# Attention in chunks and a gated feed-forward on one core: the values product on eighths of the array, a third slot of streamed output weights, later ring loads, and a longer turn in tile two

## The chip, the cores and the metric

The kernel runs on one core of a Trainium2 chip. The time is device time in microseconds (us) of one execution: the median of three runs before the change was 960.36 us, and the runs went from 959.24 to 962.48 us. Five engines with a queue each work in parallel: TensorE (PE in the profile, with its weight loads as PEld), VectorE (DVE), ScalarE (ACT), GpSimd (POOL) and SyncE (SP), which here issues nearly every DMA transfer, in the order of its own queue.

## The reference

```python
# q, k, v: (8, 8, 576, 64), batch, heads, tokens, head dim
q_c = q.reshape(B, H, nc, 64, D)                 # chunks of 64 tokens
scores = scale * (q_c @ k_c.T)                   # 64 x 64 in each chunk and head
attn = softmax(scores)                           # over the 64 keys of the chunk
x = (attn @ v_c) -> (4608 tokens, 512)           # heads side by side
xn = x / sqrt(mean(x * x) + 1e-06) * rms_g
out = (silu(xn @ w_gate) * (xn @ w_val)) @ w_out # 512 -> 1536 -> 512, fp32
```

## The kernel before

There are 4608 tokens, in nine tiles of 512. Attention works in units of 256 tokens, two to a tile. A unit has two halves of 128 tokens (two chunks of 64), called subs below.

The feed-forward is done in split fp32: each operand is a high and a low part, and a product is three matmuls. One matmul of 128 x 128 weights on 512 columns is the kernel's unit of work on TensorE. Tiles 0 to 2 go through `gated` and `down` for each of 12 blocks of the hidden width: 24 matmuls of the up products and 12 of the down product a block. The last six tiles go in three pairs (b = 0, 1, 2). A pair's up products are done in seven part products on weights streamed from DRAM in a ring of three slots (`wr` from `wsd`, `ring_load_ahead`); then its down products run over 12 steps n, each with one streamed megabyte of output weights (`wo` from `wod`, `out_load`), which feeds 24 matmuls. All these slots, the hidden values `g`, the operands `xp` and the ring, come from one pool of 18 buffers.

Attention for later tiles is spread between the feed-forward's matmuls. The order on TensorE is written out by hand from tile 1 on, as numbered steps; the order on the other engines is set by a scheduler from the order of the code and priorities. A unit's steps are: load, scores and softmax (`turned_softmax`), sums and the first half of a turn (`turned_sum`, `turn`), the second half (`turn_back`), values and norm (`turned_values`, `turned_norm`), and the turn of the result to the feed-forward's layout (`turn_x`, `turn_x_back`). `UNIT_STEPS` and `PAIR_STEPS` say how many steps each stands behind the unit's first. In tiles 1 and 2 there are two steps a block (one before the down product of the block before, one behind it).

A turn makes the softmax weights `e` (tokens on partitions) into `eT` (keys on partitions), which the values product needs as its weights: VectorE transposes blocks of 32 x 32 in place, one DMA writes `e` to DRAM (`away_e`), and four DMAs a sub read it back in another order (eight a unit).

`e` is stored as (partition, half of the keys, 32 keys, 8 heads), so that for one head neighbouring keys lie 8 elements apart, and `eT` as (partition, 64 queries, 8 heads). The values product takes one head, one chunk of 64 queries and one sub at a time: 64 keys by 64 queries as weights, 64 columns of values, on a quarter of the array (64 rows by 64 columns), 32 products a unit. An fp32 product shows in the profile as two records, so a unit shows 64.

Tile 1, the second one, is called tile two here. Beside its units 4 and 5 it computes the sums of up weights that the part products need: `load` (`w` from `wfd`), `sums` on GpSimd (line 541), `split` (casts on ScalarE, line 569, subtractions on VectorE, line 571), and stores (`wsd` from `side` and `w`). At its end `x_split` (lines 442 and 443) makes the operands `xh` and `xl` of the next tile out of `x`, which units 4 and 5 have written.

Of the kernel before, what the change touches and what calls it, by code (L numbers as in the profile page):

```python
# [8 lines left out]
F32 = mybir.dt.float32  # L9
# [5 lines left out]
ALU = mybir.AluOpType  # L15
AX = mybir.AxisListType

P = 128
CH = 64
D = 64  # L20
H = 8
# [12 lines left out]
AHEAD = 4  # L34
EARLY = 3
AHEAD_R = 3

URGENT = 300
UNIT_AT = 1, 5, 9, 13
UNIT_STEPS = -2, 0, 1, 3, 5, 6, 7  # L40
PAIR_STEPS = -4, 0, 3, 5, 8, 11, 13
CONVS = (2,), (0, 2)
Q = 32
# [4 lines left out]
NB = (NT - PLAIN) // 2  # L48
# [13 lines left out]
def tile_chunk_attn_swiglu(  # L62
# [10 lines left out]
    nc = tc.nc  # L73
# [6 lines left out]
    att = ctx.enter_context(tc.tile_pool(name="att", bufs=2))  # L80
# [118 lines left out]
    state = {}  # L199
# [95 lines left out]

    def turned_softmax(i):
        st = state[i]
        e = st["e"] = att.tile([P, 2, Q, H], F32, tag="e", name="e")
        ev = e.rearrange("p t k (a j) -> p j a t k", j=2)
        mx = small.tile([P, 2, NPAIR, 1], F32, name="mx")  # L300
        for j in range(2):
            nc.vector.tensor_reduce(mx[:, j], st["s"][j], axis=AX.X, op=ALU.max)
            nc.vector.tensor_tensor(
                ev[:, j],
                st["s"][j].rearrange("p a (t k) -> p a t k", t=2),
                mx[:, j].rearrange("p a (o i) -> p a o i", i=1).broadcast_to([P, NPAIR, 2, Q]),
                op=ALU.subtract,
            )
        nc.scalar.activation(e, e, AF.Exp, scale=SCALE)

    def turned_sum(i):
        st = state[i]
        rs = st["rs"] = small.tile([P, H, 1], F32, name="rs")
        nc.vector.tensor_reduce(rs, st["e"].rearrange("p t k h -> p h t k"), axis=AX.XY, op=ALU.add)
        nc.vector.tensor_scalar_add(rs, rs, 1e-9)
        nc.vector.reciprocal(rs, rs)

# [2 lines left out]
    def turn(i):  # L320
        st, s = state[i], i % 2
        if s == 0:
            state["eT", i // 2] = [att.tile([P, 2 * Q, H], F32, tag="eT", name="eT") for _ in range(2)]
        eT = state["eT", i // 2]
        e = st["e"].rearrange("p t k h -> p t h k")
        nc.vector.transpose(e, e)
        away = st["away"] = dram.tile([P, 2 * Q * H], F32, name=f"away_e{i}")
        nc.sync.dma_start(away, st["e"].rearrange("p t k h -> p (t k h)"))

    def turn_back(i):  # L330
        st, s = state[i], i % 2
        eT, away = state["eT", i // 2], st["away"]
        back = away.rearrange("(c t p) (k r) -> c k p t r", c=2, t=2, k=2)
        for c in range(2):
            for k in range(2):
                dst = slice((2 * s + k) * Q, (2 * s + k + 1) * Q)
                nc.sync.dma_start(eT[c][dst].rearrange("p (t q) h -> p t (q h)", t=2), back[c, k])

    def turned_values(u):
        subs = [state[2 * u + s] for s in range(2)]
        for st in subs:
            st["o"] = bank(ps_a, "ps_o")
        vt = subs[0]["v"].rearrange("p a n d -> p (a n d)").rearrange("p (c h d) -> p c h d", c=2, d=D)
        eT = state.pop(("eT", u))
        for s, st in enumerate(subs):
            st["eT"] = eT[s]
        for h in range(H):
            for c in range(2):  # L350
                for s, st in enumerate(subs):
                    rows = slice(s * CH, (s + 1) * CH)
                    nc.tensor.matmul(  # L353
                        st["o"][c * CH : (c + 1) * CH, h * D : (h + 1) * D],
                        eT[c][rows, :, h],
                        vt[rows, c, h],
                        start=True,
                        stop=True,
                    )

    def turned_norm(i):
        st = state.pop(i)
        if i % 2 == 0:

            state["xu", i // 2] = io.tile([P, 4, NDT, 2, Q], F32, tag="io", name="xu")
        xs = state["xu", i // 2].rearrange("p q a s d -> p s (q a) d")[:, i % 2]
        nc.vector.tensor_tensor(
            xs.rearrange("p (h b) d -> p h b d", b=2),
            st["o"].rearrange("p (h b d) -> p h b d", b=2, d=Q),
            st["rs"].rearrange("p h (o i) -> p h o i", i=1).broadcast_to([P, H, 2, Q]),  # L370
            op=ALU.mult,
        )

        spent = st["eT"].rearrange("p q h -> p (q h)").rearrange("p (n d) -> p n d", d=Q)
        nc.scalar.mul(xs, xs, inv_rms(xs, spent))


# [427 lines left out]
    o = two_banks(ps_h, "ps_o")  # L805
# [25 lines left out]
    for t in range(PLAIN):  # L831
        if t == 1:
            ordered = tc.manual_schedule(engines={mybir.EngineType.PE})
            ordered.__enter__()
            at = {}
            for n, u in enumerate((4, 5)):
                for k, f in enumerate(unit_steps(u, x)):
                    at.setdefault(2 + 9 * n + UNIT_STEPS[k], []).append(f)
            half = Steps(at)
            st = last.open("st", 1)  # L840
            made = [[] for _ in range(NF + 2)]
            for i in range(NPR):
                steps = sides(i, st)
                made[max(2 * i - 1, 0)].append(steps[0])
                made[2 * i].append(steps[1])
                made[2 * i + 1].append(steps[2])
        elif t == 2:
            st = last.open("st2", 1)
            x2 = st.tile([P, NSUB, DM], F32, tag="x2", bufs=1, name="x2")
            at = {}  # L850
            for n, u in enumerate(range(2 * PLAIN, 2 * PLAIN + 4)):
                for k, f in enumerate(unit_steps(u, (x, x2)[n // 2])):
                    at.setdefault(max(UNIT_AT[n] + UNIT_STEPS[k], 0), []).append(f)
            x_first, x_both = x_sides(x, x2, st)
            for n, f in enumerate(x_first):
                at.setdefault(15 + n, []).append(f)
            for n, f in enumerate(x_both):
                at.setdefault(22 + n // 6, []).append(f)
            at.setdefault(14, []).append(lambda: ring_load_ahead(0))
            half = Steps(at)  # L860
        acc = [ps_acc.tile([P, DM], F32, tag="acc", name=f"acc{s}") for s in range(NSUB)]
        prev = None
        for f in range(NF):
            g = gated(f, CONVS[f % 2], conv_step)
            if t == 0:
                if f in (0, 5):
                    u = 2 + (f == 5)
                    load_unit(u)
                    sc = two_banks(ps_a, "ps_s")
                    for i in (2 * u, 2 * u + 1):  # L870
                        scores(i, sc)
                    for i in (2 * u, 2 * u + 1):
                        softmax_rows(i)
                elif f in (2, 7):
                    for i in (2 * u, 2 * u + 1):
                        att_transpose(i)
                elif f in (3, 8):
                    o = two_banks(ps_a, "ps_o")
                    for i in (2 * u, 2 * u + 1):
                        att_values(i, o)  # L880
                    for i in (2 * u, 2 * u + 1):
                        norm(i)
                if f == NF - 1:
                    x_transpose((0, 1))
            elif t == 1 and f == NF - 1:
                for dt in range(NDT):
                    x_split(dt, blocks(x)[:, :, dt], slice(0, TT))
            if t == 1:
                if f % 2 == 0:
                    save_plain(f // 2)  # L890
                for todo in made.pop(0):
                    todo()
            if t:
                half()
            if prev is not None:
                down(acc, f - 1, *prev)
            if t:
                half()
            prev = g
        if t == 0:  # L900
            x_transpose((2, 3))
        down(acc, NF - 1, *prev)
        for s in range(NSUB):
            evacuate(acc, t, s)

    for b in range(NB):
# [25 lines left out]
        for n, (h, i) in enumerate(order):  # L932
            if i == 0:

                acc = [bank(ps_h if h and s < 2 else ps_acc, f"acc{s}") for s in range(NSUB)]
            for k in range(n, min(n + 2, len(order))):
                if k not in wos:
                    wos[k] = out_load(order[k][1])
            if n == 1 and b + 1 < NB:
                ring_load_ahead(0)  # L940
            for j in range(2):
                split_next(2 * n + j + 1)
# [60 lines left out]
```

## Time and profile before

| | |
|---|---|
| median of 3 runs | 960.36 us |
| the profiled execution | 961.05 us, of which the profile's span is 959.3 us |
| TensorE busy | 922.0 us (96%) |
| VectorE, ScalarE, GpSimd busy | 547.9, 432.4, 172.9 us |
| DMA | 231.72 MB, 242 GB/s over the span |
| matmuls with 512 columns | 3672 |

A group row of the profile gives line, engine, operation, what is written from what, shapes, the count, then busy time and mean time of one, then the engine's idle time just ahead of these instructions with what ended it. A row of the chain or the timeline begins with the start and the duration in us. SPq rows are the times that the DMA queue needed to issue, not the transfers. Starts of TensorE records that follow each other closely are closer than their durations, since they are pipelined; the time that a burst costs is read from its first start to the first start behind it.

### The profile page before, as it was taken

To read this page: it belongs to the slowest core of one execution; us is meant where nothing else is said; L and a number is where in the kernel's file an instruction comes from. 1 tells how busy PE (TensorE), PEld (TensorE's weight loads), DVE (VectorE), ACT (ScalarE), POOL (GpSimd) and SP (SyncE) were. 2 spreads that over 40 slices of the span, in tenths; PEclk is the share of its full clock that TensorE was granted. 3 is DMA by queue.
4 is the path that set the end of the run, shared out by engine and by line. 5 is a ranking of instruction groups with operands and counts; after the bars stand their busy time and mean duration, and the time that the engine had idled before them with its cause. 6 is when DMAs were issued, how large, how long until landed. Compare 5 with 4: busy or idle time off the path is not lost.

```text
span 959.3 us, 15557 instructions
## 1 busy us (share of the span) xinstructions
PE 922.0 (96%) x6040; PEld 754.7 (79%) x6040; DVE 547.9 (57%) x889; ACT 432.4 (45%) x697; POOL 172.9 (18%) x157
## 2 busy tenths in 40 slices
PE   5699999998999999999999999999999999999998
PEld 4478788886888888888887788888786888888886
DVE  5899965673557655765673735557647333233232
ACT  4998954452446643553453424445424322222222
POOL 0100012342200000233341002323330004223100
PEclk9999999998999999999999999999999999999999
DMA  8698998877775544668789756576887666436611
GB/s 335 236 349 300 338 349 319 258 239 241 220 254 182 166 148 165 250 212 286 237 289 354 252 217 263 201 255 217 299 309 301 220 259 231 168 132 266 259 45 45
DMA packets 78730, 231.72 MB, mean 242 GB/s; under 512 B 8384, under 2 KB 40128, under 8 KB 62912
## 3 DMA queue, kind: packets, MB, share of 16 engines
q1 hardware_dynamic: 78656, 230.72, 67.7%
q8 instruction: 48, 0.79, 0.3%
q14 instruction: 26, 0.21, 0.1%
HBM read 171.97 MB, written 58.72 MB: 240 GB/s over the span
## 4 chain that ended last, share of the span: by engine, by line
PE 80%; ACT 6%; DMA 6%; DVE 4%; issue 1%; SPq 1%; POOL 0%; ACTq 0%; DVEq 0%; POOLq 0%
PE acc L503 26%; PE ps_b L634 10%; PE ps_c L634 10%; PE ps_a L634 10%; PE ps_g L468 8%; PE ps_v L468 7%; PE ps_d L634 5%; PE ps_o L353 3%; DMA wo<-wod 2%; PE ps_s L237 2%; DMA wfd<-w 1%; ACT w L150 1%; DMA vt<-v_dram 1%; ACT e L273 1%; ACT raw L151 1%
## 5 line engine op out<-in xcount | busy, mean ns | idle before, releaser
L503 PE MATMUL acc<-wo,gh 128*128 128x512 f32 x576 | 179.2, 392 | 4.7 <-DMA wo<-wod 4.7
L503 PEld LDWEIGHTS acc<-wo,gh 128*128 128x128 f32 x576 | 108.5, 189 | 28.6 <-ACT xp L582 5.1
L503 PE MATMUL acc<-wo,gl 128*128 128x512 f32 x288 | 113.4, 394 | 0.3 <-DVE gl L737 0.3
L737 DVE TENSOR_TENSOR gl<-g,gh 128x512 fp32r<-128x512 f32 x72 | 49.7, 690 | 105.2 <-ACT gh L736 103.2
L634 PE MATMUL ps_c<-xp,wr 128*128 128x512 f32 x432 | 104.4, 391 | 1.1 <-DMA wr<-wsd 1.1
L634 PE MATMUL ps_b<-xp,wr 128*128 128x512 f32 x432 | 104.6, 391 | 0.0
L634 PE MATMUL ps_a<-xp,wr 128*128 128x512 f32 x432 | 103.5, 390 | 0.0
L468 PE MATMUL ps_g<-xh,parts 128*128 128x512 f32 x288 | 97.1, 396 | 1.8 <-ACT sg L486 1.4
L736 ACT CAST gh<-g 128x512 fp32r<-128x512 f32 x72 | 44.8, 622 | 118.7 <-PE acc L503 113.4
L468 PE MATMUL ps_v<-xh,parts 128*128 128x512 f32 x288 | 95.8, 392 | 0.0
L634 PEld LDWEIGHTS ps_c<-xp,wr 128*128 128x128 f32 x432 | 80.7, 188 | 18.4 <-issue 1.5
L634 PEld LDWEIGHTS ps_a<-xp,wr 128*128 128x128 f32 x432 | 80.9, 188 | 16.9
L634 PEld LDWEIGHTS ps_b<-xp,wr 128*128 128x128 f32 x432 | 80.6, 188 | 17.0
L503 PE MATMUL acc<-parts,gh 128*128 128x512 f32 x288 | 91.5, 399 | 0.0
L708 POOL TENSOR_TENSOR g<-u,u 128x512 f32<-128x512 f32 x18 | 23.2, 1288 | 349.6 <-DVE u L704 207.1
L420 POOL TENSOR_TENSOR ri<-ss,mhalf 128x1 f32<-128x1 f32 x36 | 23.6, 664 | 252.6 <-DVE ss L418 252.3
L468 PEld LDWEIGHTS ps_g<-xh,parts 128*128 128x128 f32 x288 | 54.3, 189 | 14.3 <-ACT sg L486 1.8
L503 PEld LDWEIGHTS acc<-wo,gl 128*128 128x128 f32 x288 | 54.4, 189 | 13.5 <-DVE gl L737 1.9
L468 PEld LDWEIGHTS ps_v<-xh,parts 128*128 128x128 f32 x288 | 54.5, 189 | 11.4
L503 PEld LDWEIGHTS acc<-parts,gh 128*128 128x128 f32 x288 | 54.2, 191 | 11.4
L503 PE MATMUL acc<-parts,gl 128*128 128x512 f32 x144 | 57.2, 397 | 0.0
L468 PE MATMUL ps_g<-xl,parts 128*128 128x512 f32 x144 | 56.4, 392 | 0.0
(105 smaller groups left out, 1454.1 us busy)
## 6 DMA issues: line engine op xcount, KB each, us to landing
wr<-wsd SPq DMA_DIRECT2D x63, 1024.0 KB, 7.2
wo<-wod SPq DMA_DIRECT2D x36, 1024.0 KB, 7.7
raw<-w_up_dram SPq DMA_DIRECT2D x12, 1024.0 KB, 9.5
vt<-v_dram SPq DMA_DIRECT2D x18, 512.0 KB, 6.5
wsd<-parts SPq DMA_DIRECT2D x18, 512.0 KB, 6.8
out_dram<-o SPq DMA_DIRECT2D x36, 256.0 KB, 2.7
qt<-qT_dram SPq DMA_DIRECT2D x17, 512.0 KB, 6.5
kt<-kT_dram SPq DMA_DIRECT2D x17, 512.0 KB, 6.6
```

The costliest lines, as they stand in the source:

```text
L150: nc.scalar.activation(w, high.bitcast(F32), AF.Abs, scale=2.0**16)
L151: nc.scalar.mul(low, low.bitcast(U32), 2.0**-29)
L237: nc.tensor.matmul(st["s"][j][c * CH : (c + 1) * CH, pr], st["q"][rows, pr, tok : tok + CH], st["k"][rows, pr, tok : tok + CH], start=True ...
L273: nc.scalar.activation(e[:, pr, j], st["s"][j][:, pr], AF.Exp, scale=SCALE, bias=mx[:, j, pr], accum_out=rs[:, pr, j],)
L353: nc.tensor.matmul(st["o"][c * CH : (c + 1) * CH, h * D : (h + 1) * D], eT[c][rows, :, h], vt[rows, c, h], start=True, stop=True,)
L420: nc.gpsimd.tensor_tensor(ri, ss, mhalf, op=ALU.pow)
L468: nc.tensor.matmul(ps, a[f][:, cols], b[dt], start=(dt == 0 and i == 0), stop=(dt == NDT - 1 and i == 2),)
L503: nc.tensor.matmul(acc[s], a[:, cols], b, start=(f == 0 and i == 0), stop=(f == NF - 1 and i == 2),)
L634: nc.tensor.matmul(ps, w[:, a, m, cols], xp[:, b, kt], start=start and kt == 0 and i == 0, stop=stop and kt == 1 and i == 2, skip_group_ch ...
L708: nc.gpsimd.tensor_tensor(g[:, 0, 1], kp["u2"], kept[0]["u2"], op=mult)
L736: nc.scalar.copy(gh, src)
L737: nc.vector.tensor_tensor(gl, src, gh.bitcast(F32), op=ALU.subtract)
```

## The change

Four edits:

- The layouts of `e` and `eT` become (partition, half, 8 heads, 32), so that the 32 elements of one head are neighbours for the subtraction, the sum, the transposition and the weight load. The values product takes 32 queries at a time instead of 64, on an eighth of the array (64 rows by 32 columns): 64 products a unit.
- `AHEAD_O`: at step n of the down products the loads of output weights up to step n + 2 are written, before n + 1.
- The first loads of the next pair's ring are written at step 9 of the down products, before at step 1.
- `FIRST_STEPS`: in tile two, values, turn of the result and its way back stand two steps later.

```diff
+AHEAD_O = 3
 UNIT_STEPS = -2, 0, 1, 3, 5, 6, 7
+FIRST_STEPS = -2, 0, 1, 3, 7, 8, 9
...
     def turned_softmax(i):
-        e = st["e"] = att.tile([P, 2, Q, H], F32, tag="e", name="e")
-        ev = e.rearrange("p t k (a j) -> p j a t k", j=2)
+        e = st["e"] = att.tile([P, 2, H, Q], F32, tag="e", name="e")
+        ev = e.rearrange("p t (a j) k -> p j a t k", j=2)
...
     def turned_sum(i):
-        nc.vector.tensor_reduce(rs, st["e"].rearrange("p t k h -> p h t k"), axis=AX.XY, op=ALU.add)
+        nc.vector.tensor_reduce(rs, st["e"].rearrange("p t h k -> p h t k"), axis=AX.XY, op=ALU.add)
...
     def turn(i):
-            state["eT", i // 2] = [att.tile([P, 2 * Q, H], F32, tag="eT", name="eT") for _ in range(2)]
+            state["eT", i // 2] = [att.tile([P, 2, H, Q], F32, tag="eT", name="eT") for _ in range(2)]
-        e = st["e"].rearrange("p t k h -> p t h k")
+        e = st["e"].rearrange("p t h k -> p (t h) k")
         nc.vector.transpose(e, e)
...
     def turned_values(u):
         for h in range(H):
-            for c in range(2):
-                for s, st in enumerate(subs):
-                    rows = slice(s * CH, (s + 1) * CH)
-                    nc.tensor.matmul(
-                        st["o"][c * CH : (c + 1) * CH, h * D : (h + 1) * D],
-                        eT[c][rows, :, h],
+            for t in range(2):
+                for c in range(2):
+                    for s, st in enumerate(subs):
+                        rows = slice(s * CH, (s + 1) * CH)
+                        nc.tensor.matmul(
+                            st["o"][(2 * c + t) * Q : (2 * c + t + 1) * Q, h * D : (h + 1) * D],
+                            eT[c][rows, t, h],
                             vt[rows, c, h],
...
-                    at.setdefault(2 + 9 * n + UNIT_STEPS[k], []).append(f)
+                    at.setdefault(2 + 9 * n + FIRST_STEPS[k], []).append(f)
...
-            for k in range(n, min(n + 2, len(order))):
+            for k in range(n, min(n + AHEAD_O, len(order))):
                 if k not in wos:
                     wos[k] = out_load(order[k][1])
-            if n == 1 and b + 1 < NB:
+            if n == len(order) - AHEAD_R and b + 1 < NB:
                 ring_load_ahead(0)
```

First place: SyncE's queue in tile two, around the turn of unit 5. `away_e` is its write to DRAM, `eT<-away_e` its way back, `wsd` the stores of one group of summed weights. Before:

```order
L328 DMA away_e_2148<-e 128x512
L546 DMA w<-wfd_136 128x1024
L337 DMA eT<-away_e_2148 32x2x256
L328 DMA away_e_2155<-e 128x512
L337 DMA eT<-away_e_2148 32x2x256 x3
L337 DMA eT<-away_e_2155 32x2x256
L570 DMA wsd_153<-side 128x512
```

Now:

```order
L575 DMA wsd_152<-w 128x2x256
L549 DMA w<-wfd_137 128x1024
L339 DMA eT<-away_e_2180 32x2x256 x4
L339 DMA eT<-away_e_2187 32x2x256 x4
L549 DMA w<-wfd_138 128x1024
```

Before, five of the eight loads of `eT` stood ahead of the stores `wsd_153` to `wsd_152` and three behind them; now all eight stand behind the last of these stores. The stores themselves are the same eight.

Second place: ScalarE's queue at the end of tile two. `L442` (now `L445`) is the high part of `x_split`, `side<-w` are the casts of the last group of summed weights. Before:

```order
L486 ACTIVATE sg<-ps_g 128x512
L569 CAST side<-w 128x512
L442 ACTIVATE xh_119<-x,g_col 128x512
L442 ACTIVATE xh_120<-x,g_col 128x512
L442 ACTIVATE xh_121<-x,g_col 128x512
L442 ACTIVATE xh_122<-x,g_col 128x512
L569 CAST side<-w 128x512
L491 CAST gh<-sg 128x512
L569 CAST side<-w 128x512 x2
```

Now:

```order
L489 ACTIVATE sg<-ps_g 128x512
L572 CAST side<-w 128x512 x3
L494 CAST gh<-sg 128x512
L572 CAST side<-w 128x512
L445 ACTIVATE xh_119<-x,g_col 128x512
L445 ACTIVATE xh_120<-x,g_col 128x512
L445 ACTIVATE xh_121<-x,g_col 128x512
L445 ACTIVATE xh_122<-x,g_col 128x512
```

One of the four casts stood ahead of `x_split`; now all four and the cast `gh` of the last block do.

Third place: SyncE's queue at the beginning of the first pair's down products. `wo` are the output weights by their number in DRAM (161 to 166, twice), `wr` the ring of the next pair. Before:

```order
L742 DMA wo<-wod_162 128x2048
L742 DMA wo<-wod_163 128x2048
L626 DMA wr<-wsd_140 128x2048
L626 DMA wr<-wsd_141 128x2048
L626 DMA wr<-wsd_142 128x2048
L384 DMA away_x_5094<-xu 128x1024
L742 DMA wo<-wod_164 128x2048
L391 DMA x_2578<-away_x_5094 32x4x256 x4
L742 DMA wo<-wod_165 128x2048
```

Now (from the second load on, and then the end of the same phase's loads):

```order
L745 DMA wo<-wod_162 128x2048
L745 DMA wo<-wod_163 128x2048
L745 DMA wo<-wod_164 128x2048
L745 DMA wo<-wod_165 128x2048
L387 DMA away_x_5410<-xu 128x1024
L745 DMA wo<-wod_166 128x2048
L394 DMA x_2642<-away_x_5410 32x4x256 x4
```

```order
L733 DMA out_dram<-o 128x512 x4
L745 DMA wo<-wod_165 128x2048
L745 DMA wo<-wod_166 128x2048
L629 DMA wr<-wsd_140 128x2048
L629 DMA wr<-wsd_141 128x2048
L629 DMA wr<-wsd_142 128x2048
```

Two loads of output weights stood ahead of `away_x` and three ring loads with them; now four loads of output weights do, and the ring loads stand behind all twelve of the phase.

More of the change, by code (lines that the diff above doesn't have):

```diff
@@ L322, in turn @@
         if s == 0:
-            state["eT", i // 2] = [att.tile([P, 2 * Q, H], F32, tag="eT", name="eT") for _ in range(2)]
+            state["eT", i // 2] = [att.tile([P, 2, H, Q], F32, tag="eT", name="eT") for _ in range(2)]
         eT = state["eT", i // 2]
-        e = st["e"].rearrange("p t k h -> p t h k")
+        e = st["e"].rearrange("p t h k -> p (t h) k")
         nc.vector.transpose(e, e)
         away = st["away"] = dram.tile([P, 2 * Q * H], F32, name=f"away_e{i}")
-        nc.sync.dma_start(away, st["e"].rearrange("p t k h -> p (t k h)"))
+        nc.sync.dma_start(away, st["e"].rearrange("p t h k -> p (t h k)"))
     def turn_back(i):
@@ L336, in turn_back @@
                 dst = slice((2 * s + k) * Q, (2 * s + k + 1) * Q)
-                nc.sync.dma_start(eT[c][dst].rearrange("p (t q) h -> p t (q h)", t=2), back[c, k])
+                nc.sync.dma_start(eT[c][dst].rearrange("p t h q -> p t (h q)"), back[c, k])
     def turned_values(u):
@@ L349, in turned_values @@
         for h in range(H):
-            for c in range(2):
-                for s, st in enumerate(subs):
-                    rows = slice(s * CH, (s + 1) * CH)
-                    nc.tensor.matmul(
-                        st["o"][c * CH : (c + 1) * CH, h * D : (h + 1) * D],
-                        eT[c][rows, :, h],
[L356 to L359, printed above, removed]
+            for t in range(2):
[5 more added lines that the diff above has]
+                            eT[c][rows, t, h],
+                            vt[rows, c, h],
+                            start=True,
+                            stop=True,
+                        )
     def turned_norm(i):
@@ L372, in turned_norm @@
         )
-        spent = st["eT"].rearrange("p q h -> p (q h)").rearrange("p (n d) -> p n d", d=Q)
+        spent = st["eT"].rearrange("p t h q -> p (t h) q")
         nc.scalar.mul(xs, xs, inv_rms(xs, spent))
```

## Prediction

> **What bounds the kernel now.** I read the page's shares first, then its chain that ended last, then the groups with their idle time, and then the timeline at each place where TensorE waited.
>
> ```profile
> PE 922.0 (96%) x6040; PEld 754.7 (79%) x6040; DVE 547.9 (57%) x889; ACT 432.4 (45%) x697; POOL 172.9 (18%) x157
> DMA packets 78730, 231.72 MB, mean 242 GB/s; under 512 B 8384, under 2 KB 40128, under 8 KB 62912
> PE 80%; ACT 6%; DMA 6%; DVE 4%; issue 1%; SPq 1%; POOL 0%; ACTq 0%; DVEq 0%; POOLq 0%
> 889.49 65.29 PE acc L503 x288
> ```
>
> TensorE carries 80% of the chain. The last row, from the chain in order of time, shows its pace with nothing in the way: 65.29 / 288 = 0.2267 us a matmul, which this change doesn't touch. So a gain must come from TensorE's other work, or from the few waits for DMA (6% of the chain). The values product is such other work. It and the score product stand here in the groups by form, then in the timeline, each with the row behind it:
>
> ```profile
> L353 PE MATMUL ps_o<-vt,eT 64*64 64x64 f32 x896 | 31.8, 287 | 3.5 <-DMA eT<-away_e 3.5
> L353 PEld LDWEIGHTS ps_o<-vt,eT 64*64 64x64 f32 x896 | 29.6, 213 | 8.7 <-issue 7.9 <-PE acc L503 0.7
> L237 PE MATMUL ps_s<-kt,qt 64*64 64x64 f32 x1088 | 21.2, 227 | 0.0
> L237 PEld LDWEIGHTS ps_s<-kt,qt 64*64 64x64 f32 x1088 | 18.7, 139 | 6.0 <-issue 5.6 <-DVE e L251 0.3
> ...
> 183.31 2.15 PE L353 MATMUL ps_o<-vt,eT 64*64 64x64 f32 x64
> 185.40 0.50 PE L468 MATMUL ps_g<-xh,parts 128*128 128x512 f32 x1
> ...
> 306.90 1.16 PE L237 MATMUL ps_s<-kt,qt 64*64 64x64 f32 x64
> 307.99 0.50 PE L468 MATMUL ps_g<-xh,parts 128*128 128x512 f32 x1
> ```
>
> Both bursts are 64 records of 64 x 64 weights on 64 columns, spread over the same four quarters of the array. The score burst takes 307.99 - 306.90 = 1.09 us, the values burst 185.40 - 183.31 = 2.09. The one difference in form is that the scores' weights are neighbours in memory, while `eT`'s lie 8 elements apart; and the weight load is what is longer, 213 against 139 ns. There are 14 values bursts.
>
> **Waits of TensorE that the other edits touch.** From the waits, the chain in order of time, and the timeline around the longest one:
>
> ```profile
> PE ps_o L353 <- DMA eT<-away_e: 3.5, 1, 3.5
> PE acc L503 <- DMA wo<-wod: 4.7, 3, 2.4
> PE ps_c L634 <- DMA wr<-wsd: 1.1, 1, 1.1
> ...
> 225.02 0.45 PE L353 MATMUL ps_o<-vt,eT 64*64 64x64 f32 x2
> 229.01 2.61 PE L353 MATMUL ps_o<-vt,eT 64*64 64x64 f32 x62 [3.54 <-DMA eT<-away_e]
> 231.55 1.22 PE L503 MATMUL acc<-parts,gh 128*128 128x512 f32 x2
> ...
> 231.62 4.78 PE acc L503 x12
> 336.46 2.95 PE acc L503 x12
> 524.57 7.11 PE acc L503 x23
> ```
>
> In tile two the values burst of unit 5 began at 225.02 and `eT` was there only at 229.0; the burst took 231.55 - 225.02 = 6.53 us. The 12 matmuls behind it took 4.78 us, against 2.95 for 12 behind an ordinary burst: after the wait TensorE ran slower for a while. In the pairs it waited three times for output weights, 4.7 us, and after the longest of these 23 matmuls took 7.11 us where 23 x 0.2267 = 5.2.
>
> **The change, part by part.**
>
> 1. *Values product.* Removed: 14 bursts of 64 records with strided weights. Added: 14 bursts of 128 records with 32 neighbouring weight columns, each on its own eighth. No row has such a tile. If the eight eighths run at once as the four quarters do, each eighth has 128 / 8 = 16 records in turn, as each quarter has 64 / 4 = 16 in the score burst, on the same 64 columns with a weight load half as wide: 1.09 us. Bounds: below, half the score burst, 0.55 us, if the width of the load were all that counts; above, each record at what a strided one costs now, 2.09 / 64 = 32.7 ns, so 4.18 us. I take 1.09, since the score row is nearest in form, and it shows a record begun every 1.09 / 64 = 17 ns in the whole burst; 128 at that pace without more overlap would be 2.18. Gain 14 x (2.09 - 1.09) = 14.0 us, all on the path.
>
> 2. *Strides on VectorE.* The subtraction, the sum and the transposition now touch neighbours. The rows with the same sizes and neighbouring elements:
>
> ```profile
> L303 DVE TENSOR_TENSOR e<-ps_s,mx 128x256 f32<-128x256 f32 x56 | 31.8, 655 | 0.0
> L251 DVE TENSOR_TENSOR e<-ps_s,mx 128x256 f32<-128x256 f32 x8 | 3.1, 416 | 0.0
> L314 DVE TENSOR_REDUCE rs<-e 128x8 f32<-128x512 f32 x28 | 31.2, 1117 | 2.8 <-ACT e L309 2.7
> L259 DVE TENSOR_REDUCE rs<-e 128x8 f32<-128x512 f32 x4 | 2.7, 684 | 0.6 <-ACT e L254 0.4
> L326 DVE STREAM_TRANSPOSE e<-e 128x512 f32<-128x512 f32 x28 | 33.6, 1202 | 0.0
> L381 DVE STREAM_TRANSPOSE xu<-xu 128x1024 f32<-128x1024 f32 x14 | 17.4, 1246 | 17.4 <-ACT xu L375 17.4
> ...
> 661.92 3.80 SPq L328 DMA_DIRECT2D away_e<-e  x2
> 665.77 0.42 SPq L626 DMA_DIRECT2D wr<-wsd  x1
> ```
>
> A unit saves 4 x 239 + 2 x 433 + 2 x (1202 - 1246 / 2) ns = 3.0 us, all units 41 us of VectorE's 547.9. Nothing of it is on the path, where I count it as 0; but `away_e` leaves 2 to 3 us sooner. That covers the one wait for `wr` (1.1 us): in the queue this ring load stands right behind two `away_e`, as the last two rows show. I count 1.1 us.
>
> 3. *Two steps more in tile two.* Two steps are one block, 36 matmuls, 36 x 0.2267 = 8.2 us. Without the wait the burst would find `eT` 8.2 - 4.0 = 4.2 us early, if the loads come as before. They do not quite: all eight now stand behind the eight `wsd` stores (the order shows it; three did before).
>
> ```profile
> 223.36 1.65 SPq L337 DMA_DIRECT2D eT<-away_e  x3
> ...
> 251.15 5.73 POOL L541 TENSOR_TENSOR w<-w 128x512 f32<-128x512 f32 x4 [15.95 <-DMA x<-away_x]
> 256.56 2.56 ACT L442 ACTIVATE xh<-x,g_col 128x512 fp32r<-128x512 f32 x4
> 258.18 5.75 PE acc L503 x24
> ```
>
> Three loads took 1.65 us to issue, so eight take about 4.4, until 227.8, and the last lands as the last of the three did, some 4 us after its issue, near 231.8. TensorE asks at 225.0 + 8.2 less the 1.0 that unit 4's burst saves, so at 232.2. It just fits. Gain: (6.53 - 2.09) + (4.78 - 2.95) = 6.3 us. Not free: unit 5's `x` comes later while tile two ends sooner. Its cover is the two down products behind the tile's last up product (from 258.18 on), 24 x 0.2267 = 5.4 us, against 2.56 us for the high parts; what if that cover is gone stands under the rivals.
>
> 4. *Third slot and later ring.* At the first wait the queue shows why the load was late:
>
> ```profile
> 501.36 0.85 SPq L742 DMA_DIRECT2D wo<-wod  x2
> 502.30 1.73 SPq L626 DMA_DIRECT2D wr<-wsd  x3
> 513.87 0.32 SPq L384 DMA_DIRECT2D away_x<-xu  x1
> 514.28 0.39 SPq L742 DMA_DIRECT2D wo<-wod  x1
> 520.05 1.74 SPq L391 DMA_DIRECT2D x<-away_x  x4
> ```
>
> Three ring loads went out ahead of the fourth `wo`, which then stood behind `away_x` (VectorE's work) until 514.28; TensorE waited 2.4 us for it, until 524.57. Now the fourth and fifth `wo` go out in the ring loads' place, 11 us sooner, and the sixth has two steps (2 x 24 x 0.2267 = 10.9 us) more. All three waits go: 4.7 us and the slow stretch, 7.11 - 5.2 = 1.9; together 6.6. The ring loads now stand behind the outputs of the sixth step; from there to the next up product are six steps, 6 x 5.44 = 32.6 us, in which two `wo` and three `wr`, 5 MB, need 21 us at the mean rate of 242 GB/s. I count 0; if that cover were too short, the first up product would wait for what lies over it.
>
> Sum: 14.0 + 1.1 + 6.3 + 6.6 = 28.0 us. The profiled execution took 961.05 us (span 959.3), so 933.0; it lies 0.7 over the median of 960.36, so 932.4 against that median.
>
> **The rivals.**
>
> *Four at a time.* The eighths do not all run at once, and 128 records take twice 64: 2.18 us. Then part 1 loses 14 x 0.09 = 1.3 us instead of gaining 14.0: 932.4 + 15.3 = 947.7. For it: no row shows more than four parts of the array at work, nor a stretch of more than 64 such records. Against it: the rows of the two bursts differ by the load alone, so each part seems to be held up by its own load. The Trainium skill, in "TensorEngine Tiling (Array Packing)", section Tiling Modes, lists 64 x 32 as eight independent tiles; by that the four-at-a-time case falls away, but no run here shows it.
>
> *Slower: a price by the record.* If a record keeps its 32.7 ns whatever its width, the burst is 4.18 us, the values lose 14 x 2.09 = 29.3 and the total is 932.4 + 14.0 + 29.3 = 975.7. It decides from a burst of 2.09 + 14.0 / 14 = 3.09 us on, 24 ns a record. Against it: the score row has 17 ns. The Trainium skill, "TensorE: Matmul & The Clock Gate", section "Wait — 56ns, not 53.3ns?", says that starts never come closer than about 25 ns however small the matmul. By that the burst would be 3.2 us and the whole no gain, about 962. The trace disagrees for products on different parts of the array, with 64 in 1.09 us.
>
> *Tile two hands its wait on.* In the new order all four casts of the last sums stand ahead of `x_split` on ScalarE. These sums on GpSimd ended at 251.15 + 5.73 = 256.9, and tile two's last up product would now end at 258.2 - 1.0 - 6.3 = 250.9. If the sums do not come forward, the casts begin at 256.9, just when the down products end (250.9 + 5.4), and the first matmul of the next tile waits some 3 us, at most the 6.3 gained: 935 to 939. For it: the order. Against it: these sums wait for stores and loads that the long wait itself held back.
>
> *The streamed weights wait elsewhere.* The edit only moves the wait, say to the ring: 932.4 + 6.6 = 939.0. Against it is the 32.6 us above.
>
> **How the numbers follow.** The forecast (eight at once, the waits gone) has a chance of 0.55, with a range of its own from 928 to 936 (1.09 us is known to some tenths, times 14). Four at a time 0.25, at 944 to 949; tile two or the streamed weights 0.13, 935 to 940; a price by the record 0.07, 955 to 976. 928 to 948 holds all but the last and part of the second, over 0.8. A measurement of this kernel tells 0.3% (2.9 us) from no change: the first three cases, 0.93, are faster; of the last, 0.03 falls within it and 0.04 is slower.
>
> **What the profile after would show.** The values burst from first start to the row behind it: 1.1 us if eight run at once, 2.2 if four, over 3 if the record is what costs. Of VectorE's rows the subtraction near 416, the sum near 684, the transposition near 620 ns. No wait of TensorE for `wo`, `wr` or `eT` over 1 us. A wait behind tile two's down products, ended by `x_split`, would show the third rival. The prediction is wrong above all if the burst does not shorten, since half of the sum hangs on it.

## The result, and the profile after

The changed kernel takes 936.16 us (median of four runs, 935.10 to 937.04) where the kernel before took 959.80 us on the same chip: a ratio of 0.9755, 95% interval 0.9722 to 0.9788. That is 3.8 us above the 932.4 us forecast. The profiled execution took 936.39 us. From the head of its page, the span and the engines' busy time:

```profile
span 934.6 us, 17360 instructions
...
PE 905.9 (97%) x6936; PEld 742.2 (79%) x6936; DVE 516.2 (55%) x889; ACT 431.5 (46%) x697; POOL 172.7 (18%) x157
```

The groups of the values product and of the turn (the line numbers are two or three higher than before):

```profile
L356 PE MATMUL ps_o<-vt,eT 64*32 64x64 f32 x1792 | 21.3, 225 | 1.3 <-DMA eT<-away_e 1.3
L305 DVE TENSOR_TENSOR e<-ps_s,mx 128x256 f32<-128x256 f32 x56 | 20.8, 412 | 0.0
L328 DVE STREAM_TRANSPOSE e<-e 128x512 f32<-128x512 f32 x28 | 19.7, 703 | 0.0
L356 PEld LDWEIGHTS ps_o<-vt,eT 64*32 64x32 f32 x1792 | 18.8, 105 | 6.5 <-issue 5.5 <-PE acc L506 0.7 <-DMA eT<-away_e 0.3
L316 DVE TENSOR_REDUCE rs<-e 128x8 f32<-128x512 f32 x28 | 18.7, 668 | 6.5 <-ACT e L311 6.4
```

All that TensorE waited for from 36 us on, just ahead of the first up matmul (what, for what, us in total, times, longest):

```profile
PE ps_x L462 <- ACT x L438: 2.6, 1, 2.6
PE ps_t L292 <- ACT e L275: 2.0, 2, 1.6
PE ps_g L471 <- ACT sg L489: 1.4, 1, 1.4
PE ps_o L356 <- DMA eT<-away_e: 1.3, 2, 1.1
PE ps_g L471 <- ACT xh L445: 0.5, 1, 0.5
```

The waits for `wo` (4.7 us), for `wr` (1.1) and tile two's 3.5 us for `eT` are gone. A wait for `eT` of 1.3 us stands in a new place. TensorE's timeline, an ordinary values burst and that of unit 7:

```profile
191.83 1.48 PE L356 MATMUL ps_o<-vt,eT 64*32 64x64 f32 x128
193.24 0.50 PE L471 MATMUL ps_g<-xh,parts 128*128 128x512 f32 x1
...
305.45 0.30 PE L356 MATMUL ps_o<-vt,eT 64*32 64x64 f32 x2
306.86 0.30 PE L356 MATMUL ps_o<-vt,eT 64*32 64x64 f32 x4 [1.12 <-DMA eT<-away_e]
307.32 1.43 PE L356 MATMUL ps_o<-vt,eT 64*32 64x64 f32 x122 [0.16 <-DMA eT<-away_e]
308.68 0.50 PE L506 MATMUL acc<-parts,gh 128*128 128x512 f32 x1
```

A burst, from its first start to the row behind it, takes 193.24 - 191.83 = 1.41 us in 13 of 14 places: neither the 1.09 forecast nor the 2.18 or 4.18 of two rivals. It now shows 128 records, two for each of its 64 products. Unit 7's takes 3.23 us. SyncE's queue says why:

```profile
294.79 1.76 SPq L339 DMA_DIRECT2D eT<-away_e  x3
299.07 0.35 SPq L209 DMA_DIRECT2D vt<-v_dram  x1
299.47 1.85 SPq L394 DMA_DIRECT2D x<-away_x  x4
301.37 1.37 SPq L339 DMA_DIRECT2D eT<-away_e  x3
```

The last three of unit 7's eight loads stand behind unit 8's `vt`, which held the queue 2.5 us until `away_x` had left the buffer that it reuses, and behind four loads of `x`.

### The profile page after: what moved, and what is told of

Read it like the earlier page. It is cut to its first block, busy times and chain, and to the rows that moved or that the text cites. A ratio compares the mean times of both kernels' runs of the same rounds, so it can differ in the third digit from the quotient of the medians.

```text
span 934.6 us, 17360 instructions
## 1 busy us (share of the span) xinstructions
PE 905.9 (97%) x6936; PEld 742.2 (79%) x6936; DVE 516.2 (55%) x889; ACT 431.5 (46%) x697; POOL 172.7 (18%) x157
## 4 chain that ended last, share of the span: by engine, by line
PE 85%; ACT 7%; DVE 4%; DMA 2%; issue 1%; SPq 1%; POOL 0%; ACTq 0%; DVEq 0%; POOLq 0%
PE acc L506 29%; PE ps_b L637 11%; PE ps_c L637 11%; PE ps_a L637 11%; PE ps_g L471 7%; PE ps_v L471 7%; PE ps_d L637 5%; PE ps_o L356 2%; PE ps_s L239 2%; ACT w L152 1%; ACT e L275 1%; ACT raw L153 1%; ACT parts L177 1%; DVE parts L185 1%; DMA x<-kT_dram 1%
```

## The experiments

All change the changed kernel ("the change") and were timed in five rounds beside the kernel before. Each interval is about 0.0023 wide to either side, 2.2 us, so differences under some 3 us between two of them are not told apart by the times; the profiles tell them.

| run | median, us | ratio to before (95%) |
|---|---|---|
| the change | 936.16 | 0.9755 (0.9722 to 0.9788) |
| e1, products on quarters | 930.09 | 0.9702 (0.9677 to 0.9728) |
| e2, eighths, old layout | 939.32 | 0.9796 (0.9773 to 0.9819) |
| e3, half the moving columns | 935.51 | 0.9751 (0.9727 to 0.9775) |
| e10, e1 with half the moving columns | 929.35 | 0.9691 (0.9674 to 0.9709) |
| e4, `eT` loads ahead | 935.92 | 0.9762 (0.9740 to 0.9784) |
| e5, tile two's steps back | 939.44 | 0.9803 (0.9781 to 0.9825) |
| e6, two slots, late ring | 935.20 | 0.9758 (0.9736 to 0.9780) |
| e7, three slots, early ring | 947.72 | 0.9892 (0.9873 to 0.9910) |
| e9, two slots, early ring | 942.09 | 0.9827 (0.9807 to 0.9847) |
| e8, quarters, `eT` by head | 953.15 | 0.9944 (0.9925 to 0.9964) |
| e11, pairs on quarters | 944.19 | 0.9841 (0.9821 to 0.9861) |
| e12, two units of a pair on quarters | 933.55 | 0.9742 (0.9719 to 0.9765) |

**e1: quarters again, with neighbouring columns.**

```diff
-            for t in range(2):
...
-                            st["o"][(2 * c + t) * Q : (2 * c + t + 1) * Q, h * D : (h + 1) * D],
-                            eT[c][rows, t, h],
+                        st["o"][c * CH : (c + 1) * CH, h * D : (h + 1) * D],
+                        eT[c][rows].rearrange("p t h q -> p (t h q)")[:, h * CH : (h + 1) * CH],
```

> The changed kernel with its values product back on quarters of the array: 64 products a unit, each with 64 neighbouring weight columns. Which columns these are is left aside: two heads' queries take each other's place in them, so only the time counts. Theory A (the stride of the weights was what the old burst paid for, and the new one pays for its number of records): the burst takes what the score burst takes, 1.09 us, against 1.413 on eighths; 14 x 0.32 = 4.5 us less than the changed kernel, 936.2 - 4.5 = 931.7 us. Rival B (eight eighths at once are what shortened it, the stride costs nothing): 2.09 us as in the kernel before, 14 x 0.67 = 9.4 us more than the changed kernel, 945.6 us.

TensorE's timeline, the same burst as above:

```profile
191.41 1.16 PE L355 MATMUL ps_o<-vt,eT 64*64 64x64 f32 x64
192.50 0.50 PE L470 MATMUL ps_g<-xh,parts 128*128 128x512 f32 x1
```

1.09 us, as theory A had it, and 6.1 us off the time: 4.5 from the bursts, 1.8 since unit 7's wait did not occur here, less 0.7 that unit 8's burst took longer (1.77 us). So the layout carries the whole gain of the burst, and the eighths take a third of it back.

**e2: eighths with the old layout.** `e` and `eT` have the old order again in all steps of the turn.

```diff
-        e = st["e"] = att.tile([P, 2, H, Q], F32, tag="e", name="e")
+        e = st["e"] = att.tile([P, 2, Q, H], F32, tag="e", name="e")
...
-                            eT[c][rows, t, h],
+                            eT[c][rows, t, :, h],
```

> The changed kernel with its products on eighths, but with the old layout: the 32 weight columns of a product lie 32 bytes apart. Theory A: a strided load costs by its columns, half of the old 30 ns for half the columns, so 128 of them take about 2.1 us as 64 did before; 14 x 0.67 = 9.4 us more than the changed kernel, 945.6 us, and VectorE's subtraction is back at 655 ns. Rival B (the stride costs nothing, eighths do): 1.41 us, 936.2 us. Rival C (a strided load has a fixed price by the record): up to 4.2 us, 14 x 2.8 = 39 us more, 975 us.

```profile
191.22 1.65 PE L356 MATMUL ps_o<-vt,eT 64*32 64x64 f32 x128
192.80 0.50 PE L471 MATMUL ps_g<-xh,parts 128*128 128x512 f32 x1
```

1.58 us, between theory A's 2.1 and rival B's 1.41; neither number was right. With before and e1 it fills a square of bursts:

| | columns 32 bytes apart | neighbouring columns |
|---|---|---|
| 64 records on quarters | 2.09 us (before) | 1.09 us (e1) |
| 128 records on eighths | 1.58 us (e2) | 1.41 us (the change) |

Eighths help where the stride costs (0.50 us) and hurt where it doesn't (0.32 us). The whole is 3.2 us slower than the change, 14 x 0.17 = 2.4 of it the bursts. No wait for `wr` came back, although VectorE's operations were as long as before.

**e3 and e10: half the moving columns**, on eighths and on quarters.

```diff
-                            vt[rows, c, h],
+                            vt[rows, c, h, :Q],
```

> The changed kernel with 32 instead of 64 moving columns in each of the 128 products (the second half of each head's values is left out; the normalization reads the first half twice). Theory A1 (the 1.413 us burst is set by how fast records begin, about 8.3 ns each, and not by the work within an eighth): 128 x 8.3 ns and the same beginning and end, 1.35 to 1.41 us, total 935.5 to 936.2 us. Rival A2 (each eighth is busy with its 16 products in turn, so columns set the burst): each round of eight falls by 32 columns at 2.4 GHz-like pace of the 512-column matmul, 0.2267 / 16 = 14 ns, 16 x 14 = 0.23 us less: about 1.19 us, 14 x 0.23 = 3.2 us less, 933 us.

> The kernel of e1 (64 products on quarters, neighbouring columns) with 32 instead of 64 moving columns in each product; the second half of each head's values is left out and the first is read twice, and the queries are in e1's order. Theory (a part of the array takes a load and its moving columns in turn: 58 ns a round of four, 28 of them for 64 columns at 0.2267 / 512 us each; on eighths the beginning of a record every 8.3 ns is the longer one, 67 ns a round): here 58 - 14 = 44 ns a round, burst 1.09 - 16 x 0.014 = 0.86 us, 930.1 - 14 x 0.23 = 926.9 us. Rival (the loads of the four parts go one after another, 14.5 ns for 64 columns, and the moving columns lie beside them): the burst stays at 1.07 to 1.09 us, 930 us.

The timelines of e3 and then of e10:

```profile
191.03 1.29 PE L356 MATMUL ps_o<-vt,eT 64*32 64x32 f32 x128
192.25 0.50 PE L471 MATMUL ps_g<-xh,parts 128*128 128x512 f32 x1
```

```profile
191.99 1.14 PE L355 MATMUL ps_o<-vt,eT 64*64 64x32 f32 x64
193.05 0.50 PE L470 MATMUL ps_g<-xh,parts 128*128 128x512 f32 x1
```

On quarters the moving columns count next to nothing: 1.065 against 1.091 us, so the rival held and my theory of a part's load and columns in turn fell. In the single records of the trace sixteen weight loads take 233 ns there, 14.6 ns each, in e1 and e10 alike. On eighths halving the columns saves 0.19 us (1.22 us), near rival A2's number; and the loads then begin evenly from the 49th on, sixteen in 133 to 134 ns, 8.3 ns each on average. Two loads of 32 columns thus take 16.7 ns where one of 64 takes 14.6. With 64 moving columns, in the changed kernel, the sixteens from the 49th on take about 133 and 180 ns in turn; what holds up every second one is open.

The whole of e3 is only 0.7 us faster than the change where 14 x 0.19 = 2.7 would follow: unit 7's burst took 4.07 us there, 1.97 of it one wait for `eT`, and the matmuls behind it were slow.

**e4: unit 7's loads ahead**, by a higher priority in the scheduler for the loads of units 6 to 9.

```diff
-                nc.sync.dma_start(eT[c][dst].rearrange("p t h q -> p t (h q)"), back[c, k])
+                with urgent() if 12 <= i < 20 else ExitStack(): nc.sync.dma_start(eT[c][dst].rearrange("p t h q -> p t (h q)"), back[c, k])
```

> The changed kernel with the eight eT loads of units 6 to 9 put ahead in SP's queue: for unit 7 they stand before the load of unit 8's vt, which waited 2.5 us for away_x, and before the four x loads, instead of behind them. Theory: the burst of unit 7 then finds eT and takes 1.41 us instead of 3.23, 1.8 us less: 934.4 us, with no wait for eT over 0.3 us. Rival: the loads were late by the transfers themselves and not by their place in the queue, or the wait goes to x of that unit or to vt of the next: 936.2 us.

SyncE's queue at that place, all waits of TensorE from 36 us on, and unit 7's burst:

```profile
295.13 2.16 SPq L339 DMA_DIRECT2D eT<-away_e  x4
297.39 0.37 SPq L209 DMA_DIRECT2D vt<-v_dram  x1
297.80 1.93 SPq L394 DMA_DIRECT2D x<-away_x  x4
```

```profile
PE ps_x L462 <- ACT x L438: 2.6, 1, 2.6
PE ps_t L292 <- ACT e L275: 2.1, 2, 1.5
PE ps_g L471 <- ACT sg L489: 1.3, 1, 1.3
PE ps_c L637 <- DMA wr<-wsd: 0.7, 1, 0.7
PE ps_g L471 <- ACT xh L445: 0.5, 1, 0.5
PE ps_s L239 <- issue: 0.5, 1, 0.5
```

```profile
305.79 1.48 PE L356 MATMUL ps_o<-vt,eT 64*32 64x64 f32 x128
307.20 0.50 PE L506 MATMUL acc<-parts,gh 128*128 128x512 f32 x1
```

The cause of that wait is shown: with the loads ahead, the burst takes 1.41 us. The gain is not: waits of 0.7 us for `wr` and 0.5 us ahead of a score burst took its place, and the time is the same.

**e5: tile two's steps back.**

```diff
-                    at.setdefault(2 + 9 * n + FIRST_STEPS[k], []).append(f)
+                    at.setdefault(2 + 9 * n + UNIT_STEPS[k], []).append(f)
```

> The changed kernel with the old steps for units 4 and 5 in tile two (UNIT_STEPS instead of FIRST_STEPS), all else kept. Theory: the two steps are what took the wait away; unit 5's burst waits again for eT, 3.5 us or a little more since TensorE now asks about a microsecond sooner, and the matmuls behind it run slow for 1.8 us: 936.2 + 6 = 942 us. Rival: VectorE's shorter turn (3.0 us a unit) already brings the eT loads forward far enough; a wait under 1.5 us and no slow stretch, 936 to 938 us.

```profile
223.90 0.31 PE L356 MATMUL ps_o<-vt,eT 64*32 64x64 f32 x6
226.66 1.43 PE L356 MATMUL ps_o<-vt,eT 64*32 64x64 f32 x122 [2.46 <-DMA eT<-away_e]
228.02 0.73 PE L506 MATMUL acc<-parts,gh 128*128 128x512 f32 x2
228.59 0.39 PE L506 MATMUL acc<-parts,gl 128*128 128x512 f32 x1
```

The wait is back, but with 2.5 us instead of 3.5, and the matmuls behind it keep their pace (12 of them in 2.86 us). The steps are worth 3.3 us by the times, little more than these tell apart, and 3.9 by the stretch between the score bursts on either side: not 6, but between theory and rival.

**e6, e7, e9: the square of slots and ring.** The first edit is e6, the second e7, both together e9.

```diff
-AHEAD_O = 3
+AHEAD_O = 2
...
-            if n == len(order) - AHEAD_R and b + 1 < NB:
+            if n == 1 and b + 1 < NB:
```

> The changed kernel with two slots of streamed output weights instead of three; the ring is still loaded late. Theory (the third slot is needed once the ring is late): the last wo of a pair now goes out behind the three ring loads, 4 MB in all or some 15 us at the mean rate of 250 GB/s, where TensorE gives it two steps, 10.9 us; a wait of 3 to 5 us in each of the two pairs that load a ring, 942 to 946 us. Rival (the ring's place alone was the fault): no wait over 1 us, 936.2 us.

> The changed kernel with three slots but the ring loaded early again, behind the fourth wo. Theory (the third slot alone is enough): each wo goes out a step sooner, 5.4 us, which is more than any of the old waits (2.4 us at most); no wait for wo over 0.5 us, 936.2 us. Rival (the ring's place is what counts): the fifth wo, behind three ring loads and away_x, is late as the fourth was, 2.4 and 1.9 us and slow matmuls behind: 940 to 943 us.

> The changed kernel with both parts of the streamed weights' edit undone: two slots and the early ring, as in the kernel before, all else kept. With e6 and e7 it fills the square of slots (two, three) and ring (early, late), of which 936.2 (three, late), 935.2 (two, late) and 947.7 us (three, early) are known. Theory (the ring's place is the whole gain, and a third slot with an early ring costs more than either): the waits for wo are back as before, 4.7 us with 1.9 of slow matmuls behind: 942 to 944 us. Rival (the faster turn on VectorE had already freed the queue): 935 to 938 us.

| | ring early | ring late |
|---|---|---|
| two slots | 942.1 us (e9) | 935.2 us (e6) |
| three slots | 947.7 us (e7) | 936.2 us (the change) |

The ring's place is the whole gain; with the early ring the third slot costs 5.6 us, and with the late ring it makes no difference that the times tell. My theories for e6 and e7 were both wrong. The largest entry of TensorE's list of waits from 45 us on, of e9 and then of e7:

```profile
PE acc L506 <- DMA wo<-wod: 4.0, 2, 2.2
```

```profile
PE acc L506 <- DVE gl L740: 7.2, 2, 3.6
```

In e9 the old waits for `wo` are back. In e7 no `wo` is late; the wait has moved to VectorE, whose timeline there is

```profile
523.52 1.27 DVE L600 TENSOR_SCALAR x<-x,g_col 128x512 f32<-128x512 f32 x3
524.71 1.22 DVE L603 TENSOR_TENSOR t<-x,x 128x1024 f32<-128x1024 f32 x1
...
530.01 1.23 DVE L603 TENSOR_TENSOR x<-t,x 128x1024 f32<-128x1024 f32 x1
531.16 0.68 DVE L740 TENSOR_TENSOR gl<-g,gh 128x512 fp32r<-128x512 f32 x1
```

VectorE's operations on `x` now stand in one piece, 7.6 us long, ahead of `gl`, the low part that the next down product needs; in the changed kernel the longest such piece at that place is 3.9 us. Seven megabytes of `wo` and `wr` had gone out ahead of `away_x`, and the loads of `x` waited 8.8 us for it. But VectorE itself did not wait for `x` here: it is its order, which the scheduler sets, that is another. That the later loads made the scheduler choose it is likely, not shown.

**e8: quarters with the right columns, by small pieces.**

```diff
-                nc.sync.dma_start(eT[c][dst].rearrange("p t h q -> p t (h q)"), back[c, k])
+                for t in range(2):
+                    nc.sync.dma_start(eT[c][dst, :, t], back[c, k][:, t].rearrange("p (h q) -> p h q", q=Q))
...
```

> The changed kernel with the values product on quarters, and eT laid out by head with its 64 queries together, so that the 64 weight columns are neighbours and the right ones. For that the loads of eT write pieces of 32 numbers (128 bytes) instead of 256 (1 KB), and there are 16 a unit instead of 8. Theory: the burst is 1.09 us and the loads still come in time; 930 to 932 us. Rival: the small pieces make the loads late (8 more issues are 3.3 us of SP's queue a unit, and eight times the pieces), and the bursts wait: from 1 us in some units, 935 us, to 2 us in all fourteen, 958 us.

```profile
PE ps_o L356 <- DMA eT<-away_e: 13.8, 10, 2.2
```

The burst is 1.09 us where it need not wait (7 of 14), but ten waits for `eT`, 13.8 us in all, eat it: the rival. The page counts 130,699 DMA packets instead of 78,737.

**e11 and e12: quarters by a copy on GpSimd**, in all units of the pairs, and in the first two of each.

```diff
+    def in_order(u):
+        if u >= 2 * PLAIN + 4:                                  # e12: and (u - 2 * PLAIN) % 4 < 2
+            eR = state["eR", u] = [att.tile([P, H, 2, Q], F32, tag="e", name="eR") for _ in range(2)]
+            for c in range(2):
+                nc.gpsimd.tensor_copy(eR[c].rearrange("p h t q -> p t h q"), state["eT", u][c])
...
```

> A version meant to beat both: the changed kernel with two slots (e6), and in the pairs, eight of the fourteen units, the values product on quarters with the right neighbouring columns: GpSimd copies each eT into an order by head (two copies of 128x512 a unit, into the buffers of e), so that the DMA keeps its pieces of 1 KB. Theory: eight bursts at 1.09 instead of 1.41 us, the copies hidden: 935.2 - 8 x 0.32 = 932.6 us. Rival: the copies (about 1.4 us each, by GpSimd's sums of that size) come behind the last eT and the bursts wait for them, or the next unit's e waits for its buffer: from 0.3 us a unit on nothing is gained, 935 to 940 us.

> The version of e11, with quarters and GpSimd's copies only in the first two units of each pair, where e11 showed no wait for the copies; the other ten units stay on eighths, and there are two slots (e6). Theory: four bursts at 1.09 instead of 1.41 us and nothing waits: e6's 935.2 - 4 x 0.32 = 933.9 us. Rival: the waits of e11 in the third and fourth unit came from e's buffers or from the queues as a whole, not from the copies of those units; then they stay, 2.7 us in each pair: 939 us or more.

In e11, TensorE in the third unit of a pair, and GpSimd just ahead of it:

```profile
464.13 0.33 PE L367 MATMUL ps_o<-vt,eR 64*64 64x64 f32 x4 [2.75 <-POOL eR L347]
```

```profile
462.26 1.27 POOL L722 TENSOR_TENSOR g<-u,u 128x512 f32<-128x512 f32 x1 [11.26 <-DMA qt<-qT_dram]
463.46 1.17 POOL L347 COPY eR<-eT 128x512 f32<-128x512 f32 x2
```

A copy takes 0.6 us, not 1.4, but both stand behind an operation that had held GpSimd's queue for 11 us. Such waits come to 6.2 us in five places, in the third and fourth units. In e12, which leaves those units on eighths, the burst is

```profile
403.75 1.16 PE L367 MATMUL ps_o<-vt,eR 64*64 64x64 f32 x64
404.84 0.97 PE L648 MATMUL ps_d<-xp,wr 128*128 128x512 f32 x3
```

1.09 us in all four units, nothing waits for the copies, and 933.55 us is the forecast's 933.9. It is the fastest kernel here that computes all of the reference; 2.6 us under the change (1.7 under e6, which has its two slots) is more than its bursts' 1.3 us, and the intervals overlap.

## Why the prediction was right, and where it was off

The forecast of "faster" held, and 936.2 us lies within 928 to 948, 0.2 us above the likeliest case's own 928 to 936. By its steps, from the two profiles (959.3 - 934.6 = 24.7 us against 28.0):

- *Values product, 14.0 us forecast, 14 x (2.085 - 1.413) = 9.4 measured.* This is the mis-sized term, 4.6 us. The failed step is the sentence that each eighth has 16 records in turn "as each quarter has", so that a round of eight takes as long as one of four. That the stride was what the old burst paid for held (e1): the 1.09 us was there to be had from the layout alone. But e1's columns aren't the right ones; with the right ones e8 and e11 paid for it with waits, and e12 has it in four units only. The eighths themselves cost 0.32 us a burst. With half the moving columns on both (e3, e10) 1.22 - 1.065 = 0.16 us of that are left: the price of 128 loads of 32 columns against 64 of 64. The other half comes with the 64 moving columns, and how is open. Neither the 2.18 us of "four at a time" nor the price of 32.7 ns occurred. The Trainium skill ("TensorEngine Tiling (Array Packing)", section Tiling Modes) lists 64 x 32 as eight independent tiles. The 1.41 us fits that, but no run shows how many eighths work at the same moment. The Trainium skill's floor of about 25 ns between starts ("TensorE: Matmul & The Clock Gate", section "Wait — 56ns, not 53.3ns?") doesn't hold for records on different parts of the array: they begin 14.6 ns apart on average on quarters (e1) and, from the 49th on, 8.3 on eighths (e3).
- *Strides on VectorE.* The subtraction (412 ns for 416) and the sum (668 for 684) came as forecast; the transposition takes 703 ns, not 620. VectorE's busy time fell by 31.7 us (some 41 forecast). The wait for `wr` went, but e2 has the old strides and no such wait either, and e4, with the new strides, waits 0.7 us for it; so that the 1.1 us came from this step isn't borne out.
- *Two steps more in tile two, 6.3 us.* The wait and the slow stretch went, and `x_split` caused no wait, so the third rival did not come. But e5 shows the steps to be worth 3.3 us in the changed kernel: without them the wait is 2.5 us there and no slow stretch follows. Which of the other edits shortened it no run tells.
- *Third slot and later ring, 6.6 us.* Undone together they cost 5.9 us (e9), near the forecast; but e9 has no slow stretch, which was 1.9 of the 6.6, so that the agreement is in part luck. The working credited both edits; e6 and e7 show the ring's place to be all of it.
- *Not foreseen:* unit 7's burst, 3.23 us where an ordinary one now takes 1.41. It was 0.7 us over an ordinary one before and is 1.8 over now, 1.1 us lost, and its wait of 1.3 us breaks the line "no wait for `eT` over 1 us". The first up matmul also began 0.7 us later than before, and what stands behind the last matmul's start is 0.6 us shorter; no part of the change explains either.

Together: between one score burst and the next, the stretch with tile two's wait is 6.6 us shorter beside its burst's 0.67, that with the wait for `wr` 1.4, and the two with the waits for `wo` 8.3 beside their bursts' 0.67 each (6.6 in the working; a short wait for `gl` and slower matmuls behind the waits had been left out). 9.4 + 6.6 + 1.4 + 8.3 + 0.6 - 1.1 - 0.7 = 24.5 us of the 24.7. So the miss of the values product was partly made up, by luck, by streamed weights that gained 1.7 us more than forecast.

The forecast named the burst as what would decide. It did shorten, by two thirds of what was forecast.

## What to carry to other kernels

Price a burst of small products by its weight loads, how many and in what layout: neighbouring columns halved the burst, and cutting each product in two then cost a third of that gain. When a change bundles an order and a buffer, fill the square of both: here the order carried all, and the buffer without it did harm. A load or copy moved in an in-order queue should be followed to what stands behind it, in the other queues too: e4 and e7 removed a wait and made another.

## What the runs showed of the hardware

- With 64 x 64 tiles a weight load that reads columns 32 bytes apart doubles the burst (2.09 against 1.09 us); with 64 x 32 tiles it adds 0.17 us.
- Records of 64 x 32 tiles can begin 8.3 ns apart on average: in e3 from the 49th of the 128 to the end of the burst.
- VectorE's transposition of 128 x 512 takes 1204 ns with the old strides in e2 and 703 ns on neighbours.
- After a wait of 3.6 us in e7 the granted clock was 0.57 over a window of four microseconds; after 2.75 us in e11 matmuls were slow as well. After 2.2 us in e9 and 2.5 us in e5 they were not, though in the kernel before they were after 2.4 us and in e3 after 2.0: the length of the wait alone doesn't decide it. In the kernel before, the granted clock was 0.96 from 190 to 280 us and 0.98 from 470 to 570 us, the stretches of its two slow passages; in the changed kernel it was 1.00 in both. The stretch in e7 (a row of the view by windows: window, its length, TensorE's busy time and count, granted clock, DMA share, GB/s):

```profile
532.00:536.00 4.00, 4.00 (x11) 0.57 0.69 248
```
